# Half of each input load moved from ScalarE's queue to GpSimd's software queue

## The chip, the cores and the metric

The kernel runs on one core of one Trainium2 chip. The metric is the device time of one execution in microseconds (us). A core has a matrix engine (TensorE, in profiles PE, with its weight loads as PEld), three engines for elementwise work (VectorE or DVE, ScalarE or ACT, GpSimd or POOL) and SyncE (SP), which here only issues DMAs. Each engine works through its own instruction stream in order. A DMA is issued by an instruction in the stream of some engine; the transfer itself is done by 16 DMA engines, which all queues share. DMAs issued by SP and ScalarE go through two hardware queues (q1 and q10 in the profile), those issued by GpSimd through a software queue (q0), for which GpSimd writes the descriptors itself.

## The reference, cut to what matters

The input x has 8 batches of 3584 tokens with 192 features. The first step is a causal convolution over 7 tokens, with one set of softmax-normalized weights for each of 8 heads of 24 features. The second step is a mixture of 8 experts: a gate gives each token 8 logits, all 28672 x 8 logits are sorted, and tokens are assigned to experts greedily from the largest logit down, each expert taking at most 3584 tokens. Each token then goes through its expert's two layers with a ReLU between them.

```
w = softmax(weight)                                  # 8 heads x 7 taps
attn[b, s] = sum_k w[h, k] * x_padded[b, s + k]      # per head of 24 features
logits = attn @ w_gate                               # 28672 x 8
for idx in argsort(-logits.flatten()):               # greedy, capacity 3584
    tok, e = idx // 8, idx % 8
    if assigned[tok] < 0 and counts[e] < cap: assigned[tok] = e; counts[e] += 1
out[tok] = relu(attn[tok] @ w1[e]) @ w2[e]
```

## The kernel before, in words

The work falls into two stages that overlap at their border. In the first, some 160 us long, x is read in 16 half batches of 1792 tokens. A half batch lies in SBUF as a tile X of 118 partitions by 16 by 192 floats: 112 partitions hold the tokens of 16 windows, and 6 more hold the tokens ahead of each window. The convolution of a head is one multiplication of TensorE by a Toeplitz matrix TH (function `conv`, tile cv in PSUM, four of them in turn), and ScalarE copies each result from PSUM into a tile a. When all 8 heads are done, ScalarE issues the store of a into a DRAM buffer attn (L214; 1344 KB). VectorE transposes a (tile aT), TensorE computes the gate's logits from it (tile pl), and ScalarE and VectorE bring them into a table LT.

Beside that, from the fourth half batch on, VectorE and TensorE search for a threshold of the logits and build the first lists of tokens (class `Route`: `thresh`, `settle`, `count`, `place`, `sort`). These steps are placed between the convolutions by a planner (`Pace`, `Meter`, `Steps.hook`) that sums costs when the program is built; the order on each engine is then fixed. In the same way the weights of the first expert are loaded into tiles raw by SP (`wload`, L1235 to L1240) and split into a high and a low part by ScalarE and VectorE (`wsplit`).

In the second stage, the rest of the time, tokens are gathered by expert with indirect DMAs of GpSimd (L1308), go through the two layers on TensorE (tiles ph and y), and are scattered to the output, again by GpSimd (L1383).

Inputs are loaded by `load` (L183 to L200). There are four buffers X, so input i takes the buffer of input i - 4. Input 0 is loaded by SP in one piece. For each other input, GpSimd clears the first six rows of an even one (L188), SP loads the six rows ahead of the windows (L189 or L192) and the first 8 of the 16 windows (L194), and the second 8 windows go into a list `later`, from which they are issued a little further on:

```
def part(eng, w, n):
    eng.dma_start(t[6:118, w:w + n], bass.AP(tensor=x.tensor, offset=o + w * W * D, ap=[[D, W], [W * D, n], [1, D]]))
...
    part(nc.sync, 0, 8)
    later.append(partial(part, A, 8, 8))
```

Here A is ScalarE, P is GpSimd, and each half is 112 partitions of 8 rows of 768 bytes, 672 KB. The main loop (L1648) loads input i + 3 ahead of the convolution of half batch i, and issues the second half at once (L1651, L1652); for input 3 it is issued in the middle of half batch 0 (L1663). Since input i + 3 takes the buffer of input i - 1, all its loads wait for the convolution that has just ended. So in ScalarE's stream stand, one after the other: the last evictions of half batch i - 1, its store, the second half of input i + 3, and the first evictions of half batch i.

GpSimd has little to do in the first stage: constants, a part of the Toeplitz matrix, the six rows of each even input, and then, before the first gather, the memset of a weight tile dl (L1192) and of xg (L1306).

Of the kernel before, what the change touches and what calls it, by code (L numbers as in the profile page):

```python
# [114 lines left out]
def build(ctx, tc, nc, x, weight, wg, attn, LT, wk):  # L115
# [4 lines left out]
    V, A, PE, P = nc.vector, nc.scalar, nc.tensor, nc.gpsimd  # L120
# [62 lines left out]
    def load(i, later=None):  # L183
        t = X[i] = k.xp[i % 4].tile([118, 16, D], F32, name="X")
        b, hf = divmod(i, 2)
        o = x.offset + (b * 3584 + hf * 1792) * D
        if hf == 0:
            P.memset(t[0:6, 0], 0.0)  # L188
            nc.sync.dma_start(t[0:6, 1:16], bass.AP(tensor=x.tensor, offset=o + (W - 6) * D,  # L189
                                                    ap=[[D, 6], [W * D, 15], [1, D]]))  # L190
        else:
            nc.sync.dma_start(t[0:6], bass.AP(tensor=x.tensor, offset=o - 6 * D, ap=[[D, 6], [W * D, 16], [1, D]]))  # L192
        def part(eng, w, n):
            eng.dma_start(t[6:118, w:w + n], bass.AP(tensor=x.tensor, offset=o + w * W * D, ap=[[D, W], [W * D, n], [1, D]]))  # L194

        if later is None:
            part(nc.sync, 0, 16)
        else:
            part(nc.sync, 0, 8)
            later.append(partial(part, A, 8, 8))  # L200

    def conv(i, mid, hold=None):
        t = X.pop(i)
# [37 lines left out]
    def logits_t(i):  # L241
# [5 lines left out]
        A.activation(o, v, AF.Copy)  # L247

    k.load, k.conv, k.transp, k.logits, k.logits_t = load, conv, transp, logits, logits_t
    k.toeplitz, k.gate_load, k.gate_ops = toeplitz, gate_load, gate_ops  # L250
    return k
# [1519 lines left out]
```

## Time and profile before

| | |
|---|---|
| median of three runs | 1243.67 us (1243.0 to 1246.95) |
| profiled execution | 1241.13 us, of which the span from the first to the last instruction is 1239.3 us |
| granted TensorE clock, mean | 0.997 |
| busy time of TensorE | 1204.1 us (97% of the span) |
| weight loads / VectorE / ScalarE / GpSimd | 1034.1 / 985.6 / 559.8 / 532.7 us |
| DMA moved | 182.00 MB, mean 147 GB/s |
| loads by L194 on SP / on ScalarE | 15 of 672 KB and one of 1344 KB / 15 of 672 KB |
| issue of a load by L194 on ScalarE | 319 to 1933 ns, median 427 |

A row of a time line reads: start in us, duration in us, engine, line, operation, tile written and tile read, partitions by elements, number of instructions merged into the row, and in brackets the idle time of the engine before it with what ended it. An engine's name with a q (ACTq, SPq) marks its queue of issues. Line 56 is that of a helper through which most instructions pass, so the tiles' names tell the operations apart; the name X is both that of the inputs and, with a number, of work tiles of the lists. The chain of waits is followed back from the last instruction: each row is what the next one waited for.

### The profile page before, as it was taken

To read this page: it belongs to the slowest core of one execution; us is meant where nothing else is said; L and a number is where in the kernel's file an instruction comes from. 1 tells how busy PE (TensorE), PEld (TensorE's weight loads), DVE (VectorE), ACT (ScalarE), POOL (GpSimd) and SP (SyncE) were. 2 spreads that over 40 slices of the span, in tenths; PEclk is the share of its full clock that TensorE was granted. 3 is DMA by queue.
4 is the path that set the end of the run, shared out by engine and by line. 5 is a ranking of instruction groups with operands and counts; after the bars stand their busy time and mean duration, and the time that the engine had idled before them with its cause. 6 is when DMAs were issued, how large, how long until landed. Compare 5 with 4: busy or idle time off the path is not lost.

```text
span 1239.3 us, 21782 instructions
## 1 busy us (share of the span) xinstructions
PE 1204.1 (97%) x7694; PEld 1034.1 (83%) x7694; DVE 985.6 (80%) x2126; ACT 559.8 (45%) x1251; POOL 532.7 (43%) x520
## 2 busy tenths in 40 slices
PE   5999899999999999999999999999999999999997
PEld 2545578889989988889888889999999999999997
DVE  7498679898998999889979866777777777777772
ACT  4544555556445455444554443343333433343332
POOL 2000234435555545555464435434534444543522
PEclk9999999999999999999999999999999999999999
DMA  9999674659426473746343442114223222413100
GB/s 244 372 344 323 193 223 123 141 174 315 146 76 214 135 238 108 238 150 190 100 130 102 129 106 74 42 39 159 93 101 105 100 98 96 154 64 132 48 23 29
DMA packets 128580, 182.00 MB, mean 147 GB/s; under 512 B 20992, under 2 KB 91088, under 8 KB 126800
## 3 DMA queue, kind: packets, MB, share of 16 engines
q1 hardware_dynamic: 85856, 104.13, 27.5%
q0 software_dynamic: 21504, 44.07, 11.9%
q10 hardware_dynamic: 21104, 32.34, 7.7%
q8 instruction: 62, 1.02, 0.3%
q14 instruction: 54, 0.44, 0.1%
HBM read 102.37 MB, written 78.12 MB: 146 GB/s over the span
## 4 chain that ended last, share of the span: by engine, by line
PE 86%; DMA 7%; DVE 4%; issue 1%; ACT 1%; SPq 0%; ACTq 0%; POOL 0%; POOLq 0%; DVEq 0%
PE ph L56 41%; PE y L56 39%; DMA X<-in_x_dram 4%; PE bg L56 3%; PE cv L56 2%; DMA attn<-a 2%; DVE TH L56 1%; PE pl L56 1%; DVE X L56 1%; DMA X<-otab 0%; DVE aT L56 0%; DVE hl L56 0%; DMA raw<-in_moe_w_dram 0%; PE px L56 0%; DMA wb<-in_weight_dram 0%
## 5 line engine op out<-in xcount | busy, mean ns | idle before, releaser
L56 PE MATMUL y<-w,hh 128*128 128x384 f32 x1792 | 535.6, 355 | 0.0
L56 ACT ACTIVATE hh<-ph 128x512 fp32r<-128x512 f32 x448 | 267.6, 597 | 458.1 <-PE ph L56 398.2
L56 PE MATMUL y<-w,hl 128*128 128x192 f32 x1792 | 448.9, 251 | 0.0
L56 DVE SCALAR_TENSOR_TENSOR hl<-ph,hh 128x512 fp32r<-128x512 f32 x448 | 307.9, 687 | 132.0 <-ACT hh L56 110.8
L56 PE MATMUL ph<-xa,w 128*128 128x512 f32 x1344 | 395.2, 402 | 0.4 <-issue 0.4
L56 PEld LDWEIGHTS y<-w,hl 128*128 128x128 f32 x1792 | 340.9, 190 | 16.2
L56 PEld LDWEIGHTS y<-w,hh 128*128 128x128 f32 x1792 | 336.3, 188 | 19.5 <-issue 1.5
L1383 POOL DMA_INDIRECT out_dram<-yo,ia x128 | 145.2, 1134 | 234.2 <-DVE yo L56 197.1
L56 PEld LDWEIGHTS ph<-xa,w 128*128 128x128 f32 x1344 | 218.4, 189 | 21.5 <-issue 2.0
L1383 POOL DMA_INDIRECT out_dram<-yo,ib x96 | 94.9, 988 | 221.0 <-DVE yo L56 213.6
L56 PE MATMUL ph<-xd,w 128*128 128x512 f32 x448 | 177.4, 396 | 0.0
L1308 POOL DMA_INDIRECT xg<-attn,ja x128 | 140.4, 1097 | 79.6 <-issue 38.5
L56 PE MATMUL ph<-xd,dl 128*128 128x512 f32 x448 | 174.2, 389 | 0.2 <-issue 0.2
L56 DVE STREAM_TRANSPOSE xs<-xg 32x128 f32<-32x128 f32 (+2 forms) x408 | 164.8, 404 | 6.6
L56 ACT ACTIVATE yt<-y 128x192 f32<-128x192 f32 x224 | 73.0, 326 | 103.1 <-PE y L56 85.0
L56 PE MATMUL cv<-X,TH 118*128 118x384 f32 x256 | 101.4, 522 | 17.8 <-DVE TH L56 11.9
L1308 POOL DMA_INDIRECT xg<-attn,jb x96 | 103.6, 1079 | 29.3 <-issue 29.3
L56 DVE TENSOR_TENSOR yo<-y,yt 128x192 f32<-128x192 f32 x224 | 79.2, 354 | 42.4 <-ACT yt L56 39.3
L56 PEld LDWEIGHTS ph<-xd,dl 128*128 128x128 f32 x448 | 84.2, 188 | 20.2 <-issue 0.5
L56 PEld LDWEIGHTS ph<-xd,w 128*128 128x128 f32 x448 | 84.0, 187 | 19.6 <-issue 0.6
L56 PEld LDWEIGHTS cv<-X,TH 118*128 118x128 f32 x256 | 45.3, 197 | 48.5 <-POOL TH L152 11.7
L56 ACT ACTIVATE a<-cv 128x384 f32<-128x384 f32 x128 | 58.2, 494 | 47.1 <-PE cv L56 15.7
(237 smaller groups left out, 919.7 us busy)
## 6 DMA issues: line engine op xcount, KB each, us to landing
attn<-a ACTq DMA_DIRECT2D x16, 1344.0 KB
raw<-in_moe_w_dram SPq DMA_DIRECT2D x56, 192.0 KB
X<-in_x_dram SPq DMA_DIRECT2D x15, 672.0 KB
X<-in_x_dram ACTq DMA_DIRECT2D x15, 672.0 KB
kw<-w SPq DMA_DIRECT2D x36, 256.0 KB
kv<-w SPq DMA_DIRECT2D x24, 384.0 KB
scr<-xs SPq DMA_DIRECT2D x96, 96.0 KB
w<-kw SPq DMA_DIRECT2D x6, 1536.0 KB
```

Of the source, the lines that this page charges most:

```text
L56: return f(*a, **k)
L1308: self.nc.gpsimd.indirect_dma_start(out=t[:, b], out_offset=None, in_=self.attn[0:rows], in_offset=bass.IndirectOffsetOnAxis(ap=idx[b], ax ...
L1383: st = self.nc.gpsimd.indirect_dma_start(out=self.out, out_offset=bass.IndirectOffsetOnAxis(ap=idx, axis=0), in_=o, in_offset=None, bounds ...
```

## The change

One line of `load` is changed. The second half of an input is issued by GpSimd on the software queue if the input's number is above 3, and by ScalarE otherwise. That concerns 12 loads, inputs 4 to 15; the halves of inputs 1, 2 and 3 stay on ScalarE. The moment of the call in the program does not change, nor do the bytes and the tiles.

```diff
             part(nc.sync, 0, 8)
-            later.append(partial(part, A, 8, 8))
+            later.append(partial(part, P if i > 3 else A, 8, 8))
```

## The prediction

> **What bounds the kernel now.** I read the busy share by slices first, then the busy time by stages, then the time lines of TensorE, ScalarE and VectorE in the first 160 us, and last the chain of waits there. The slice line and three stages (columns: PE, PEld, DVE, ACT, POOL busy, granted clock, DMA share, GB/s):
>
> ```profile
> DMA  9999674659426473746343442114223222413100
> ...
> 0.00:60.00 60.00, 44.88 (x294) 23.45 (x295) 35.52 (x91) 29.81 (x76) 11.18 (x41) 1.00 1.02 306
> 60.00:94.00 34.00, 31.32 (x266) 16.22 (x265) 31.21 (x85) 16.18 (x45) 0.69 (x2) 1.00 1.05 347
> ...
> 200.00:400.00 200.00, 198.36 (x1255) 177.47 (x1254) 180.53 (x398) 107.09 (x240) 100.07 (x86) 1.00 0.58 173
> ```
>
> From about 160 us on TensorE has hardly a gap (198.36 of 200 us), and the edited line belongs to the loading of the inputs, which is over before that. So the change can only shift the moment at which that dense stage begins; what it is worth is read before 160 us. There, three things are near full at once: TensorE, VectorE (31.21 of 34 us from 60 to 94), and the DMA engines (share 1.02 to 1.05). Next, TensorE's time line: its waits in brackets, with what ended them.
>
> ```profile
> 25.23 4.14 PE L56 MATMUL cv<-X,TH 118*128 118x384 f32 x12 [2.21 <-ACT a L56]
> ...
> 39.93 1.56 PE L56 MATMUL cv<-X,TH 118*128 118x384 f32 x4 [0.34 <-ACT a L56]
> ...
> 48.24 1.56 PE L56 MATMUL cv<-X,TH 118*128 118x384 f32 x4 [0.66 <-ACT a L56]
> ...
> 64.29 0.17 PE L56 MATMUL bg<-m_x,ones 128*128 128x24 bf16 x1 [0.80 <-DVE m_x L56]
> 64.66 1.56 PE L56 MATMUL cv<-X,TH 118*128 118x384 f32 x4 [0.19 <-ACT a L56]
> ...
> 73.44 1.56 PE L56 MATMUL cv<-X,TH 118*128 118x384 f32 x4 [0.86 <-ACT a L56]
> ...
> 81.95 1.56 PE L56 MATMUL cv<-X,TH 118*128 118x384 f32 x4 [0.83 <-ACT a L56]
> ...
> 134.19 0.91 PE L56 MATMUL cv<-X,TH 118*128 118x384 f32 x2 [0.27 <-ACT a L56]
> 135.48 0.91 PE L56 MATMUL cv<-X,TH 118*128 118x384 f32 x2 [0.38 <-ACT a L56]
> ...
> 146.14 0.33 PE L56 MATMUL pt<-ident,L 128*128 128x128 f32 x1 [2.52 <-issue]
> 146.31 3.60 PE L56 MATMUL cv<-X,TH 118*128 118x384 f32 x6
> ```
>
> TensorE has four PSUM tiles for the convolution, and it stops when ScalarE does not evict them. Why ScalarE is late stands in its own time line; L214 is the store of a half batch, L194 the second half of an input:
>
> ```profile
> 21.00 0.32 ACTq L214 DMA_DIRECT2D attn<-a  x1
> 24.32 0.32 ACTq L194 DMA_DIRECT2D X<-in_x_dram  x1
> 24.69 2.63 ACT L56 ACTIVATE a<-cv 128x384 f32<-128x384 f32 x6 [3.72 <-DMA X<-in_x_dram]
> ...
> 38.94 0.32 ACTq L194 DMA_DIRECT2D X<-in_x_dram  x1
> ...
> 44.38 0.32 ACTq L214 DMA_DIRECT2D attn<-a  x1
> ...
> 60.29 1.55 ACTq L214 DMA_DIRECT2D attn<-a  x1
> 62.17 1.84 ACTq L194 DMA_DIRECT2D X<-in_x_dram  x1
> 64.12 2.02 ACT L56 ACTIVATE a<-cv 128x384 f32<-128x384 f32 x5 [3.86 <-DVE X L56]
> ...
> 126.23 0.32 ACTq L214 DMA_DIRECT2D attn<-a  x1
> 126.59 0.60 ACT L56 ACTIVATE X<-bg 128x512 bf16<-128x512 f32 x1 [2.36 <-PE cv L56]
> ...
> 133.13 0.63 ACT L56 ACTIVATE w<-raw 128x512 fp32r<-128x512 f32 x1 [1.41 <-DMA raw<-in_moe_w_dram]
> ```
>
> Input 4's second half stands between the store of half batch 0 and the evictions of half batch 1. The store is out at 21.32, the load only at 24.32, and the evictions behind it start at 24.69. The same happens at 62.17 for input 9. What the load waits for is in the chain of waits:
>
> ```profile
> 46.03 16.06 DMA X<-in_x_dram
> 62.17 17.10 DMA X<-in_x_dram
> 79.37 1.93 ACTq L194
> ...
> 114.37 13.25 DMA attn<-a
> 127.63 5.41 DMA raw<-in_moe_w_dram
> ```
>
> The load issued at 46.03 lands at 62.09, and at 62.17 the next one goes out; that lands at 79.27, and at 79.37 the next goes out. The load does not wait for its buffer (that half batch was convolved by then) but for the landing of the load two half batches earlier. Four issues on SP and ScalarE make up a half batch, so I read this as a ring of eight outstanding hardware issues; it is an inference from the times. So ScalarE is held by the pace of the DMA engines, through an instruction that has nothing to do with its own work.
>
> **What the change takes off ScalarE.** Twelve issues (inputs 4 to 15) leave ScalarE's stream. TensorE's waits for ScalarE just behind them are 2.21 (at 25.23), 0.34, 0.66, 0.19, 0.86 and 0.83: together 5.09 us. Not all of it can be had:
>
> ```profile
> 52.32 0.38 DVE L56 TENSOR_REDUCE M<-LT 128x16 f32<-128x128 f32 x1 [4.38 <-ACT LT L56]
> ...
> 84.24 0.18 DVE L56 TENSOR_REDUCE t_mx<-bg 128x3 f32<-128x24 f32 x1 [0.53 <-PE bg L56]
> ...
> 93.96 0.37 DVE L56 TENSOR_REDUCE M<-LT 128x16 f32<-128x128 f32 x1 [0.91 <-ACT LT L56]
> ```
>
> Before 60 us VectorE idles 4 us in each half batch (4.38 at 52.32), so the first three waits, 2.21 + 0.34 + 0.66 = 3.21 us, reach the end of that stretch in full. From 60 to 94 VectorE runs the threshold search without a gap but the 0.53 at 84.24; the matmuls of that search wait for it (0.80 at 64.29). If TensorE comes earlier there, it waits for VectorE instead: of 0.19 + 0.86 + 0.83 = 1.88 us only the 0.53 is gained. The 0.91 at 93.96 becomes shorter but opens nothing, since TensorE's last count of the search was already paced by VectorE. That makes 3.74 us at 94.
>
> **What it does to the ring.** With three hardware issues a half batch instead of four, the eighth issue back is older by two thirds of a half batch, and it is another one. The last weight load went out at 127.63, when the store issued at 114.37 had landed; it kept ScalarE waiting 1.41 us at 133.13 and TensorE 0.27 + 0.38. After the change it stands eight behind a small row load of input 15, which has long landed. I count 0.65 us gained. In turn the store of half batch 12 (126.23) will stand eight behind the store of 11, which landed at 127.62: a new wait of up to 1.4 us, with evictions queued behind it on ScalarE and TensorE behind those. Below nothing it cannot be. I take 0, since ScalarE was idle 2.36 us right there (126.59) and the store of 11 no longer shares its queue with input 15's half; 1.4 stays in the range.
>
> **What it adds on GpSimd.** The profile has no plain load on the software queue. The nearest rows are its row gathers, of 128 rows of 768 B each; and, behind what is moved, GpSimd's own stream:
>
> ```profile
> L1308 POOL DMA_INDIRECT xg<-attn,ja x128: 994/1012/1995, 140.6 to 726.3; - x128
> ...
> L56 DVE TENSOR_TENSOR oa<-irep,q x64: 648/684/894, 106.6 to 724.3; 128x1024 bf16<-128x1024 bf16 x64
> ...
> 102.98 0.25 POOL L188 MEMSET X<- 6x192 f32 x1 [16.83 <-PE pt L56]
> 103.28 0.95 POOL L1192 MEMSET dl<- 64x1024 f32 x1
> ...
> 140.60 1.25 POOL L1308 DMA_INDIRECT xg<-attn,ja  x1 [35.57 <-DVE ja L56]
> ```
>
> Half an input is 112 partitions of 8 rows, 896 rows of 768 B: seven gathers' worth. The bounds are 0.3 us (an issue that costs what the hardware queue's does, 0.32) and 14 us (seven of the slowest gather, 1.995). I take 7, seven of the undisturbed 0.994, since the gather is the software queue's only row. GpSimd waits for the input buffer as ScalarE did, and it idles 16.83 us between two memsets there. Queued behind each issue are the memset of the next even input, for which SP waits with that input's first rows and first half; the memset of dl (103.28), first read in the dense stage; and the first gather, which waits for VectorE until 140.60. At 7 us an issue fits into a half batch of 8 to 9 us, and all of these keep their time: nothing on the path. Above a half batch it is otherwise; that is the rival that ends slower. VectorE beside the software queue: its oa operations stay at 684 ns in the median and 894 at most, among gathers, so I add nothing for it.
>
> **The sum.** 3.21 + 0.53 + 0.65 = 4.39 us, or 4.4, against the profiled execution: 1241.13 us (span 1239.3), so 1236.7 for a like one. The median of the three runs shown is 1243.67, 2.5 above that execution; taking the same 4.4 from it gives 1239.3. A difference within 0.3% (3.7 us) can hardly be told from none on this kernel, so the forecast lies just beyond that.
>
> **Rivals.** *The DMA engines set the pace.* They are never idle until 125 us, and nothing is taken from them. Input 4's first half was down about when the issue at 38.94 came free, and half batch 4 starts near 44.4 (store at 44.38): 5.5 us of slack. The forecast uses 2.55 of them there. Now three queues share the engines, and the first half has one third of the turns where it had one half against a load. If it slips by more than the remaining 2.9 us, TensorE waits for X itself, and the early gain of 2.21 goes: 4.4 - 2.2 = 2.2 us, 1241.5. Against it: the loads are issued up to 2 us earlier, and the stores no longer stand before them. The Trainium skill, page "DMA: Bandwidth & Descriptors", section "Issuing engines are not separate DMA queues", says that DMAs run on the same 16 engines whoever issues them, so that spreading them saves only issue time. By that rule this rival would hold, with the issue's own wait as the whole gain; the trace agrees so far that the share is above 1 with two queues.
>
> *The wait stays on ScalarE.* The store itself took 1.55 us to issue at 60.29. If it is the fullness of the queue that holds ScalarE, the store takes over the wait: nothing gained, 1243.7. Against it: at 24.32 the load's issue took 0.32 and the time went before it.
>
> *GpSimd falls behind* (slower). Twelve issues of c us from 21 us on end at 21 + 12c; input 15's half lands 17.1 us later, and half batch 15 is convolved from about 147 (in the row of 146.31), 142.6 in the forecast. It turns against the change from c = (142.6 - 21 - 17.1) / 12 = 8.7 us; each us above costs 12. At c = 10, between seven times 0.994 and seven times 1.995, this is 15.6 us: 1254.9. For it: VectorE is full from 60 on, and a gather was once stretched to 1.995. Against: the median is 1.012. The Trainium skill, page "SBUF — State Buffer", section "SBUF: two separate sides", speaks against the change here: an operation of VectorE that takes both ports locks GpSimd out of writing descriptors, and the DMA starves. By that rule c would be stretched wherever VectorE is full; the trace has the stretch, but in few gathers.
>
> **How the numbers follow.** Forecast 0.52, DMA pace 0.20, wait stays 0.13, GpSimd behind 0.15. So faster by over 0.3%: 0.52; within: 0.33; slower: 0.15. The forecast's own range is 1235 to 1240: 1240 is its edge, and 1235 is all 5.09, the 0.65 and the 2.52 us at 146.14 (all engines idle, with no releaser that I can name; I leave it) gone: 8.3 us. The whole range goes from 1235 to 1247: upwards it takes in both cases near no change, the new wait of 1.4 and the highest run of before, 1246.95. It leaves out most of the third rival and little below.
>
> **What would show it.** Right: no L194 on ScalarE after input 3; the evictions of half batch 1 start near 21.5; TensorE's 2.21 at 25.23 is gone and those at 40, 48, 73 and 82 too; VectorE without a gap from 57 to 90; the weight split without a wait for its DMA; GpSimd's issues below 8.5 us; the dense stage 4 us earlier. Wrong: matmuls waiting for a landing of X, stores with issues of 1 us and more, GpSimd busy throughout up to 110 us, or VectorE's operations longer beside GpSimd's issues.

## The result, and the profile after

The changed kernel takes 1258.82 us (median of 4 runs, 1257.29 to 1259.69), the kernel before beside it 1243.96 (1243.0 to 1246.95). The ratio is 1.0111, 95% interval 1.0099 to 1.0123: slower by 14.9 us, outside the predicted range. The profiled execution took 1259.69 us, its span 1257.9. The profiled pair differs by 18.6 us in its spans, 3.7 more than the medians, because the profiled run of before lies 2.8 us under its median and that of after 0.9 above its own.

The waits of TensorE that the change was to remove are gone. In TensorE's time line of the changed kernel (start, duration, instructions, and in brackets the idle time ahead with what ended it) the first three half batches run without the gap of 2.21 us, and the waits for ScalarE at 40, 48, 73 and 82 us have no counterpart:

```profile
19.42 7.98 PE L56 MATMUL cv<-X,TH 118*128 118x384 f32 x24 [0.37 <-DVE TH L56]
...
39.99 1.56 PE L56 MATMUL cv<-X,TH 118*128 118x384 f32 x4
...
47.33 2.90 PE L56 MATMUL cv<-X,TH 118*128 118x384 f32 x4 [5.67 <-DMA X<-in_x_dram]
...
51.17 1.89 PE L56 MATMUL cv<-X,TH 118*128 118x384 f32 x4
...
69.62 0.17 PE L56 MATMUL bg<-m_x,ones 128*128 128x24 bf16 x1 [0.80 <-DVE m_x L56]
...
150.03 0.33 PE L56 MATMUL pt<-ident,L 128*128 128x128 f32 x1 [2.46 <-ACT L L56]
...
161.74 0.97 PE L56 MATMUL ph<-xa,w 128*128 128x512 f32 x3
```

The same matmuls in TensorE's time line of before, the first of half batch 4 and the first of the dense stage:

```profile
43.50 1.45 PE L56 MATMUL cv<-X,TH 118*128 118x384 f32 x4
...
157.43 0.96 PE L56 MATMUL ph<-xa,w 128*128 128x512 f32 x3
```

TensorE arrives 2 us early at half batch 4 and then waits 5.67 us for input 4. It starts it at 47.33 instead of 43.50, and its first four matmuls take 2.90 us instead of 1.45. The stage view has the granted clock (columns as before: busy us of PE, PEld, DVE, ACT, POOL, granted clock, DMA share, GB/s):

```profile
0.00:60.00 60.00, 41.85 (x250) 21.76 (x251) 33.83 (x89) 27.97 (x67) 15.55 (x46) 0.94 0.98 287
60.00:94.00 34.00, 32.23 (x279) 16.72 (x281) 29.21 (x79) 18.03 (x46) 3.94 (x6) 1.00 1.03 341
...
45.00:50.00 5.00, 2.67 (x4) 1.17 (x4) 0.95 (x2) 0.49 (x1) 0.00 (x0) 0.51 0.99 318
```

After the pause TensorE works at about half clock for a few us (0.51 between 45 and 50 us); matched matmul by matmul it is then 6.0 us behind before. By the first matmul of the dense stage 4.3 us are left (161.74 against 157.43).

The dense stage, from there to the last matmul, lasts 1079.1 us against 1074.6. And behind the last matmul (ended at 1240.82 and 1232.02) the span runs on for 17.1 us instead of 7.2. What fills most of that time are two instructions of GpSimd's queue. They raise the software queue's semaphores at the branch that is not taken (L1740), and drain the queue (L1766). The groups of these lines, durations in ns as min/median/max, in before:

```profile
L1740 POOLq INC_SWDGE_SEM  x1: 670/670/670, 1234.1 to 1234.1; - x1
...
L1766 POOLq DRAIN  x3: 40/107/3545, 1234.8 to 1239.0; - x3
```

and in the changed kernel:

```profile
L1740 POOLq INC_SWDGE_SEM  x1: 2201/2201/2201, 1246.6 to 1246.6; - x1
...
L1766 POOLq DRAIN  x3: 46/103/8241, 1248.8 to 1257.6; - x3
```

So the spans' 18.6 us are 4.3 in the first stage, 4.5 in the dense one and 9.8 at the end. The prediction had terms for the first only.

Why was input 4 late? GpSimd's time line shows that its issues are cheap and early, input 5's half at 26.42, input 6's at 33.84:

```profile
21.83 1.10 POOL L194 DMA_DIRECT2D X<-in_x_dram  x1
26.42 0.86 POOL L194 DMA_DIRECT2D X<-in_x_dram  x1 [3.49 <-PE cv L56]
...
33.84 0.83 POOL L194 DMA_DIRECT2D X<-in_x_dram  x1
41.85 0.83 POOL L194 DMA_DIRECT2D X<-in_x_dram  x1 [7.18 <-PE pt L56]
```

SP's time line of the changed kernel, where L189 is the row load of inputs 4 and 6 and L194 their first half:

```profile
24.37 0.27 SPq L189 DMA_DIRECT2D X<-in_x_dram  x1
24.68 0.75 SPq L194 DMA_DIRECT2D X<-in_x_dram  x1
...
37.17 7.44 SPq L189 DMA_DIRECT2D X<-in_x_dram  x1
44.65 3.81 SPq L194 DMA_DIRECT2D X<-in_x_dram  x1
```

and the issues for input 4 in that of before:

```profile
20.51 0.27 SPq L189 DMA_DIRECT2D X<-in_x_dram  x1
20.83 1.22 SPq L194 DMA_DIRECT2D X<-in_x_dram  x1
```

Two things changed. Input 4's loads on SP are issued 3.9 us later. And its first half, issued at 24.68, needs 22.40 us to land by the chain of waits, at 47.08 (before: issued at 20.83, its completions end at 38.92); SP's issues grow to several us behind it. The queues between 25 and 35 us (packets, MB, share of DMA time) in before:

```profile
q10 hardware_dynamic: 1637, 2.61, 72.3%
q1 hardware_dynamic: 1418, 1.06, 34.7%
```

and in the changed kernel:

```profile
q10 hardware_dynamic: 944, 1.98, 54.0%
q0 software_dynamic: 348, 1.37, 36.4%
q1 hardware_dynamic: 576, 0.43, 14.2%
```

SP's queue q1, which carries the first halves, moves 0.43 MB instead of 1.06. Three suspects follow: the late issue, the competition of the software queue, and, at the end, the loads themselves or their number.

### The profile page after: what moved, and what is told of

Read it like the earlier page. It is cut to its first block, busy times and chain, and to the rows that moved or that the text cites. A ratio compares the mean times of both kernels' runs of the same rounds, so it can differ in the third digit from the quotient of the medians.

```text
span 1257.9 us, 21789 instructions
## 1 busy us (share of the span) xinstructions
PE 1208.0 (96%) x7694; PEld 1036.5 (82%) x7694; DVE 983.8 (78%) x2126; ACT 561.5 (45%) x1251; POOL 542.1 (43%) x532
## 4 chain that ended last, share of the span: by engine, by line
PE 84%; DVE 7%; DMA 3%; issue 2%; ACT 1%; another core or an unknown queue 0%; POOL 0%; POOLq 0%; DVEq 0%; SPq 0%
PE ph L56 39%; PE y L56 37%; PE cv L56 4%; PE bg L56 3%; DMA X<-in_x_dram 3%; DVE X L56 2%; DVE aT L56 1%; PE pl L56 1%; DVE hl L56 1%; DMA raw<-in_moe_w_dram 0%; PE px L56 0%; DVE yo L56 0%; POOL TH L152 0%; DMA wb<-in_weight_dram 0%
## 5 line engine op out<-in xcount | busy, mean ns | idle before, releaser
L56 PEld LDWEIGHTS y<-w,hl 128*128 128x128 f32 x1792 | 340.9, 190 | 16.2
L56 ACT ACTIVATE a<-cv 128x384 f32<-128x384 f32 x128 | 61.0, 490 | 46.6 <-PE cv L56 38.7
```

Source lines behind the costliest of these rows:

```text
L56: return f(*a, **k)
```

## The experiments

Each kernel was timed beside runs of before in the same batch. The level of before moved between batches (medians of 1231.7 to 1243.9 us), so times are compared within a batch. `A` is ScalarE, `P` GpSimd; the condition in the line of the change is all that differs where no other diff is shown.

**The end: number of DMAs, or loads?** In the built program the DMAs raise eight completion semaphores in turn, hardware and software DMAs eight each, and a DMA waits for the one eight places back. I shall call them lanes. Twelve more software DMAs shift the lanes by four, and that was the first theory for the longer end. `late8` has `P if i > 7 else A`; `moved_pad4` is the change, `pad4` the kernel before, each with four tiny software loads:

```diff
+            if i == 9:
+                for j in range(4):
+                    nc.gpsimd.dma_start(lst.tile([1, 8], F32, name="pad%d" % j), wg[0:1, :])
```

> Only inputs 8 to 15 move, so 8 more software DMAs than before instead of 12. Theory: the end of the program depends on the number of software DMAs modulo 8 (eight completion lanes in turn), so with 8 more the 17 us behind the last matmul fall back to the 7.3 us of before; and inputs 4 to 7 stay on ScalarE, so the wait of 5.67 us for input 4 at 47 us is gone. 1242 to 1246 us. Rival, the end is prolonged by loads on the software queue as such, whatever their number: 16 to 17 us behind the last matmul, 1252 to 1254 us.

> The change, and four loads of 32 bytes on the software queue ahead of half batch 9, into tiles that nobody reads: 16 more software DMAs than before. Theory: the end falls back to 7.3 us, the first stage stays 4 us behind; 1249 us, and 1244.5 if the 4.5 us lost between 160 and 730 us come from the lanes too. Rival, the loads as such prolong the end: 1258 us.

> The kernel before with the same four loads of 32 bytes on the software queue ahead of half batch 9, no input moved: 4 more software DMAs. Theory: the end takes 17 us instead of 7.3 with nothing else changed; 1253 to 1254 us, up to 1258 if the lanes also cost the 4.5 us between 160 and 730 us. Rival, it is the moved loads: no change, 1244 us.

Measured: `late8` 1.0049 of before (1.0030 to 1.0067), `moved_pad4` 1.0116 (1.0088 to 1.0143), `pad4` 1.0019 (1.0004 to 1.0033). The theory fell in all three. Behind the last matmul stand 10.8 us in `late8` (7.3 expected), 17.05 in `moved_pad4` (7.3 expected) and 7.6 in `pad4` (17 expected). So it is the loads. `late8` loses some 5.3 us in the medians, 3.2 of them at the end (10.8 against the 7.6 of `pad4`); the rest is not assigned. The two lines in `late8`:

```profile
L1740 POOLq INC_SWDGE_SEM  x1: 1677/1677/1677, 1238.1 to 1238.1; - x1
...
L1766 POOLq DRAIN  x3: 46/103/6117, 1239.8 to 1246.5; - x3
```

The profiled execution of `pad4` took 1253.3 us, 7 more than its median, so only its end is read from it; where the 2 us of its median lie is open.

Next came other numbers of loads, `late10` (`i > 5`) and `late11` (`i > 4`); the same loads in smaller pieces, `moved_rows`; and a longer program on GpSimd without a load, `pool_nops`, which is before with 24 memsets of 32 bytes:

```diff
-            later.append(partial(part, P if i > 3 else A, 8, 8))
+            later.append(rows if i > 3 else partial(part, A, 8, 8))
...
+        def rows():
+            for w in (8, 9):
+                P.dma_start(t[6:118, w:16:2], bass.AP(tensor=x.tensor, offset=o + w * W * D, ap=[[D, W], [2 * W * D, 4], [1, D]]))
```

> Inputs 6 to 15 move, 10 loads. The work at the end (raising the software queue's semaphores, and the drain behind it) took 4.2 us before, 7.8 us with 8 loads, 10.4 us with 12: 9.1 us expected with 10. Whether it starts only 3.8 us after the branch, behind the last scatter's landing, as with 12 loads, or at once as with 8: 15.5 or 12.1 us behind the last matmul. Inputs 4 and 5 stay on ScalarE, so no wait for input 4; 5 us slower than before with the early start, 8 with the late one.

> Inputs 5 to 15, 11 loads. The raising of the semaphores takes 2.07 us and the drain 7.7. If the late start comes with a number of rows in the software queue, it sets in here or at 12: 13 or 16.5 us behind the last matmul.

> The change, but each software load as two, of the even and of the odd windows, so that two rows of 768 bytes never lie side by side in SBUF: 24 software loads, the same bytes and the same number of rows. Theory: a packet of the software queue holds six rows because they lie side by side; now it holds one, the software queue gets no more turns' worth of bytes than SP's queue, the first half of input 4 lands earlier and TensorE's wait for it falls from 5.67 to 2 or 3 us. If the work at the end goes by rows, the 17 us behind the last matmul stay, 1255 to 1256 us in all; if it goes by software loads, they grow to 24 us, 1262 us. Rival, the packet's size has no part in it: the wait stays at 5 to 6 us.

> The kernel before, with 24 memsets of 32 bytes more on GpSimd at half batch 9, no DMA more. If the late start at the end comes from the length of GpSimd's program (the changed kernel fetched one block of instructions more), the raising of the semaphores starts 3.8 us late here too and the span's end moves 1.5 to 2 us away from the last matmul; if it comes from what lies in the software queue, it starts at once and the end takes 7.3 to 7.6 us.

`late10` measured 1.0061 (1.0043 to 1.0079; 8.4 us in the medians where 5 were expected, since a wait for an input comes on top, told below), `moved_rows` 1.0099 (1.0080 to 1.0117), and one execution each of `late11` 1240.3 us (before: 1232.57) and of `pool_nops` 1240.6 (before: 1241.85). Their ends, with those of kernels told of further below:

| kernel | software loads of an input's half | raising us | longest drain us | raising starts after the last matmul us | end us |
|---|---|---|---|---|---|
| before | 0 | 0.67 | 3.55 | 2.1 | 7.2 |
| pool_nops | 0 | 0.67 | 3.53 | 2.1 | 7.7 |
| four_pool | 1 | 0.81 | 3.40 | 2.1 | 7.5 |
| both45 | 4 | 1.18 | 4.07 | 2.1 | 8.2 |
| late8 | 8 | 1.68 | 6.12 | 2.1 | 10.8 |
| late10 | 10 | 1.94 | 7.18 | 2.1 | 12.1 |
| late11 | 11 | 2.06 | 7.67 | 2.1 | 12.7 |
| the change | 12 | 2.20 | 8.24 | 5.8 | 17.1 |
| moved_turn | 12 | 2.20 | 8.24 | 4.9 | 16.2 |
| moved_pad4 | 12, and 4 tiny ones | 2.22 | 8.32 | 5.6 | 17.1 |
| moved_rows | 24 of half the size | 2.21 | 8.32 | 5.5 | 16.9 |
| moved_and_two | 13 | 2.33 | 8.73 | 5.6 | 17.5 |
| both_pool | 24 | 2.42 | 9.22 | 5.4 | 17.9 |

Each load adds 0.13 us to the raising, (2.20 - 0.67) / 12, and from 8 to 12 loads 0.53 us to the drain, (8.24 - 6.12) / 4. Twice the loads of half the size cost the same, and four tiny loads add 0.03 us to the raising (0.70 in `pad4`), so the number of issues does not set it. The bytes alone do not either: `rows_pool`, told of below, moves only 0.15 MB more on the software queue than before and raises for 0.79 us, about as long as `four_pool` with one load of 672 KB. What it goes by is open. From 13 to 24 loads raising and drain hardly grow. With one or two loads the drain ends no later than SP's own last steps (both at 1238.4 in before) and costs nothing.

In the kernels with 12 loads and more the raising also starts 2.8 to 3.7 us late. The 9.8 us are thus about 1.5 + 4.7 + 3.7. In the changed kernel the late start is 0.2 us behind the landing of the last scatter (1246.60 and 1246.43), but in `moved_turn` the raising starts at 1233.11, ahead of that landing at 1233.66, so it does not wait for it. The cause is not settled, and it need not be the loads. TensorE's sequencer, VectorE and SP stand still at this branch in every kernel, SP for 3.5 us in before; in the six kernels with the late start GpSimd does so too. These six, the changed kernel and the last five rows of the table, are also the only ones of all the runs whose pages count 55 packets on q14, a queue that the profile calls one of instructions. In before, and in the changed kernel:

```profile
q14 instruction: 54, 0.44, 0.1%
```

```profile
q14 instruction: 55, 0.45, 0.1%
```

`pool_nops` starts at once with as many rows of GpSimd in its trace as the changed kernel, but it has 54 such packets too. So a pause for the loading of GpSimd's program is a rival that no run tested; if it holds, the 3.7 us come from where the program happens to be cut and not from the loads.

**The first stage: off ScalarE, but not on the software queue.** `on_sp` has `nc.sync if i > 3 else A`.

> The second half of inputs 4 to 15 issued by SP, behind the first half, instead of by ScalarE or GpSimd: it leaves ScalarE but stays on a hardware queue, and the count of software DMAs is that of before. Theory (the prediction's reading of the waits was right, and the software queue is what hurts): TensorE's waits for ScalarE ahead of 60 us, 3.2 us, go, no wait for input 4 takes their place, the end takes 7.3 us; 1239.5 to 1241. Rival, a load that leaves ScalarE for any other place is held up in a way that costs the same: 1243 to 1248.

Measured 1.0088 (1.0060 to 1.0115): the theory fell, the rival held, and it cost more than that said. Input 4's first half lands in time, at 39.03, but the second half, now behind it on the same queue, only at 44.34. TensorE's time line in `on_sp`:

```profile
44.59 2.77 PE L56 MATMUL cv<-X,TH 118*128 118x384 f32 x4 [3.37 <-DMA X<-in_x_dram]
...
97.08 1.53 PE L56 MATMUL cv<-X,TH 118*128 118x384 f32 x4 [2.09 <-DMA X<-in_x_dram]
...
140.26 1.65 PE L56 MATMUL cv<-X,TH 118*128 118x384 f32 x2 [6.32 <-ACT a L56]
```

The end is 7.6 us there, but SP, which now issues both halves, falls behind: two loads take it 2.8 to 6.4 us to issue, the first weight load goes out at 125.50 instead of 113.46, and ScalarE's time line shows the bill:

```profile
138.71 0.63 ACT L56 ACTIVATE w<-raw 128x512 fp32r<-128x512 f32 x1 [8.69 <-DMA raw<-in_moe_w_dram]
```

**Late issue, or competition?** SP's row load of input 4 is late in the changed kernel because it now stands eight places behind the second half of input 2, which lands at 24.3; before, ScalarE's load for input 4 stood there. `moved_turn` adds one tiny hardware load, which moves the lanes on by one. `moved_and_two` puts the second half of input 2 on the software queue as well (`P if i == 2 or i > 3 else A`).

```diff
         k.gate_load()
+        nc.sync.dma_start(lst.tile([1, 8], F32, name="turn"), wg[0:1, :])
```

> The change, and one load of 32 bytes on SP's queue just behind the gate's weights, which moves every later hardware DMA on by one completion lane. Theory: the row load of input 4 waited for the second half of an earlier input only because the two share a lane when ScalarE's issue is left out; with the lanes moved on it is issued at 20.5 to 21 us instead of 24.4, its first half lands some 3.5 us earlier, and TensorE waits about 2 us for it instead of 5.67: 1255 us. Rival, the packets of the software queue alone hold the first half up: TensorE waits as long as in the changed kernel, 1258 to 1259 us.

> The change, and the second half of input 2 on the software queue too, so that SP's loads of inputs 3 and 4 inherit no late lane and are issued at 17 to 18 and 20.5 to 21 us. If the late issue made TensorE's wait for input 4, it falls from 5.7 us to under 2, and the kernel is 3 to 4 us faster than the changed one on the same chip (ratio to before 1.008 to 1.009 instead of 1.0115). If the packets of the software queue starve the first half whenever it is issued, the wait stays at 4 us or more and the ratio at 1.011 to 1.012. The end takes 17 to 18 us in both.

`moved_turn` (1.0115, 1.0094 to 1.0137) missed its aim: the lane passed to SP's first half of input 3, issued at 24.50 instead of 18.33, and TensorE waited 9.33 us for input 3. `moved_and_two` did what it was to do. Its SP issues input 4 on time, yet the first half lands at 47.56, and TensorE waits no less:

```profile
21.27 0.27 SPq L189 DMA_DIRECT2D X<-in_x_dram  x1
21.58 0.31 SPq L194 DMA_DIRECT2D X<-in_x_dram  x1
```

```profile
47.69 2.90 PE L56 MATMUL cv<-X,TH 118*128 118x384 f32 x4 [5.87 <-DMA X<-in_x_dram]
```

The ratio is 1.0101 (1.0085 to 1.0116). So the late issue is not what makes the 5.67 us; the competition is. ScalarE's stores, which now go out earlier, are not enough for it: they go out as early in `on_sp`, where the first half, issued at 25.28 with no software load beside it, lands at 39.03. `moved_rows` was also to test the packets' size, but the edit did not change it (382 packets for 1.37 MB between 25 and 35 us, 3.6 KB each), so it says nothing on that; its waits are 1.79 us for input 3 and 4.18 for input 4. In `late10` and `late11` TensorE waits too, for the second input that moves (4.28 us for input 7, 3.93 for input 6), and in `late8` for none.

If the half on SP's queue is starved beside software loads, the wait goes when that half joins them (`both_pool`). `four_pool` has `P if i == 4 else A`.

```diff
-            part(nc.sync, 0, 8)
+            part(P if i > 3 else nc.sync, 0, 8)
```

> Both halves of inputs 4 to 15 on the software queue, only the six rows stay on SP: 24 software loads. Theory (beside software loads the hardware queue gets too small a share, so the half left on SP lands late): no half is left behind, TensorE's wait for input 4 falls from 5.7 us to under 2; the work at the end doubles, 18 us instead of 10.4, behind the late start: 24 to 26 us behind the last matmul; 1.014 to 1.016 of the time before. Rival, the loads are late because the DMA engines are full, whatever the queue: the wait stays at 4 us or more, 1.018 and up.

> Only the second half of input 4 on the software queue. Theory: one load of 672 KB outruns the first half of input 4 once, TensorE waits 2 to 5 us for it; the end takes 7.6 us; 1.002 to 1.004 of the time before. Rival, it takes the stream of software loads, with that of input 5 ahead of input 4's first half: no wait for input 4, the 2.2 us gained behind half batch 0 stay, 0.998.

`both_pool` takes 1.0064 (1.0041 to 1.0086). TensorE's waits up to 160 us there (us in all, times, longest):

```profile
PE cv L56 <- DVE TH L56: 13.2, 2, 12.2
PE cv L56 <- ACT a L56: 1.9, 1, 1.9
PE bg L56 <- DVE m_x L56: 1.4, 3, 0.8
```

No wait for an input is left, though both halves of 12 inputs ride on the software queue. It loses 7.6 us against before, but its end alone is 10.4 us longer (17.9 against 7.5 in `four_pool`, of the same batch), so the rest of it gains about 2.8. My 24 to 26 us for its end were wrong, as the work there stops growing. In `four_pool` the rival held: with one software load there is no wait for input 4, and it is the one version whose interval lies below 1, if only just: 0.9986 (0.9973 to 0.9999), 1.3 us in the medians. It takes the stream: issued at nearly the same moment (25.27 and 24.68), the first half lands at 42.04 here and at 47.08 in the changed kernel. There the software halves of inputs 5 and 6, needed some 8 and 16 us after input 4, had landed by 36.2 and 42.7 us, ahead of input 4's first half. That no wait is seen in `four_pool` is in part luck: TensorE is held for 4.03 us by ScalarE just before and would else have come to input 4 shortly before it landed. That wait is what `four_pool` loses again, and it is in ScalarE's time line, at its load of input 6, which inherits the lane of a store:

```profile
40.63 0.33 ACTq L194 DMA_DIRECT2D X<-in_x_dram  x1
41.08 1.64 ACT L56 ACTIVATE a<-cv 128x384 f32<-128x384 f32 x4 [6.72 <-DMA attn<-a]
```

**Is there a version that keeps the gain?** `four_sp`: only input 4 on SP (`nc.sync if i == 4 else A`), with the tiny load of `moved_turn`. `two_pool`: `P if i == 2 else A`. `rows_pool`: the gate's weights and the six rows of inputs 2 and 3 by GpSimd, no half moved (`P if i in (2, 3) else nc.sync` in L189 and L192, `P` in L168). `both45`: both halves of inputs 4 and 5 by GpSimd. `four_six`: `P if i in (4, 6) else A`.

> The kernel before with the small load that moves the lanes on, and only the second half of input 4 issued by SP; all else stays on ScalarE, nothing more on the software queue. Theory: the wait of TensorE for ScalarE behind half batch 0, 2.2 us, goes, row and first half of input 4 are issued as early as before, no wait for input 4 appears: 2 us faster than before, 1241.5 to 1242. Rival, SP's queue is held back by ScalarE's larger packets whatever the moment of issue: a wait for input 4 of 2 us or more takes the gain, 1243 to 1245.

> The kernel before, with only the second half of input 2 issued by GpSimd; inputs 4 to 15 stay on ScalarE. Theory: what held a load until 24.5 us was the completion lane of that half of input 2, which the eighth hardware DMA after it inherits (ScalarE's load for input 4 before, SP's row load of input 4 in the changed kernel, SP's first half of input 3 where the lanes were moved on by one). On the software queue that half holds no such lane: TensorE's wait of 2 us for ScalarE behind half batch 0 goes, no wait for an input takes its place, one software load is too few to prolong the end (7.3 us): 2 us faster than before. Rival, the wait was for the bytes and not for the lane, or the software queue's packets hold up the first half of input 2 or 3: no faster, or slower by a wait for input 2 or 3.

> The kernel before, with three small loads on the software queue instead of SP's: the gate's weights (6 KB) and the six rows of inputs 2 and 3 (72 KB each at most). No half of an input moves. The completion lane of the second half of input 2 then passes to the row load of input 5, issued at 28 us, instead of to ScalarE's load for input 4. Theory: TensorE's wait of 2 us for ScalarE behind half batch 0 goes, nothing is starved, the end takes 7.5 us: 0.998 of the time before. Rival, the next lanes hand the wait on, to ScalarE's load of input 5 or to a first half: 1.000 or above.

> Both halves of inputs 4 and 5 on the software queue, all else as before: 4 software loads. Theory: TensorE's wait of 2 us for ScalarE behind half batch 0 goes, no half is left behind a stream, so no wait for an input; ScalarE's load of input 6 inherits the lane of store 0, landed by then. The work at the end takes 5.2 us (2.55 and 4 times 0.66), about 1 us past the landing that covered it: 0.999 of the time before, between 0.998 and 1.000. Rival, the ScalarE wait comes back at a later lane, as in the kernel with only input 4 moved: 1.000 to 1.003.

> The second halves of inputs 4 and 6 on the software queue, all else on ScalarE. Theory: with only input 4 moved, ScalarE's load of input 6 inherited the lane of store 1 and TensorE waited 4 us for ScalarE at 41 us; with that load moved too nothing of ScalarE waits there, two software loads with 15 us between them do not outrun SP's queue, and the work at the end, 3.9 us, stays behind the last landing (7.5 us in all): 0.997 of the time before, faster than with input 4 alone (0.9986). Rival, input 6's software half outruns its first half or SP's row load of input 7, which now inherits store 1's lane, comes late: a wait for input 6 or 7 of 2 us or more, 0.999 to 1.002.

All five are slower: `four_sp` 1.0044 (1.0027 to 1.0060), `two_pool` 1.0022 (1.0012 to 1.0031), `rows_pool` 1.0024 (1.0006 to 1.0043), `both45` 1.0016 (1.0007 to 1.0025), `four_six` 1.0048 (1.0034 to 1.0062). The 2 us at 25 us are gained in each (also in `two_pool` and `rows_pool`, where the load for input 4 stays on ScalarE and only the place eight issues back has another owner), and a later load inherits the wait: input 3's first half in `four_sp` (TensorE waits 3.36 us), ScalarE's load of input 5 in `two_pool` and `rows_pool` (TensorE waits 4.65 and 4.72 us for the evictions behind it), input 3 and ScalarE's load of input 6 in `both45` (1.61 and 2.86). In `four_six` a second software load, issued at 33.8 us, is enough to bring back the wait for input 4 that `four_pool` does not have: the first half lands at 44.93 instead of 42.04, and TensorE, not held by ScalarE before it, is there at 41.2:

```profile
45.18 2.04 PE L56 MATMUL cv<-X,TH 118*128 118x384 f32 x4 [3.98 <-DMA X<-in_x_dram]
```

**The dense stage.** `before_again` is before, unchanged, for a second profile.

> The kernel before, unchanged, for a second profile: the first one, at 1241.1 us, lies under the median of its runs. The end takes 7.3 us again; where the dense stage is about 3 us slower than in the first profile, those 3 us are no part of the change's cost.

It took 1230.16 us, where the median of its batch was 1231.68. Its dense stage, from first ph to last matmul, lasts 1068.3 us; in the same batch it lasts 1068.2 in `moved_turn` and 1068.4 in `moved_rows`, both with all 12 halves on the software queue. So in that batch the change costs the dense stage nothing. In the batch of `pad4` and `on_sp` it lasts 1077.6 us in `on_sp` and 1079.4 in `moved_pad4`. The 4.5 us of the first pair may be scatter in the main, since its profiled runs lie 3.7 us further apart than the medians; that the scatter falls into this stage is inferred, and 0.8 us are not assigned.

## Why the prediction was wrong, point by point

Two steps failed. The forecast took it that the first half of an input would land within its slack beside the software loads, and its sum had no term for what runs behind the last matmul.

**What the change takes off ScalarE: the waits went, the gain was not kept.** The reading that TensorE waits for ScalarE, and ScalarE for a landing eight issues back, stands: every kernel whose load for input 4 left ScalarE has no gap at 25 us. In `both_pool`, where no wait for an input is left, about 2.8 us show of the 3.74 (to 94 us) that were forecast.

**"What it does to the ring" stopped half way.** It asked which wait goes when the eighth issue back changes, for two places late in the stage, and not who stands at the eighth place behind the slow load at the beginning. That was SP's row load of input 4, held till 24.37. In the changed kernel this is not what costs the time (`moved_and_two`), but such a place handed on is what undid most of the versions that were to keep the gain. The 0.65 us at the weight split came, the two waits of TensorE are gone, but not for the reason given. The last weight load did not go out early. It waited longer, for a store, as the row of SP and the line of SP's waits from 110 to 140 us in the changed kernel show:

```profile
132.43 0.47 SPq L1238 DMA_DIRECT2D raw<-in_moe_w_dram  x1
```

```profile
SPq L1238 <- DMA attn<-a: 11.4, 1, 11.4
```

That load lands 3.1 us later than before (136.13 against 133.05), in a stage that runs 4.4 us later, and ScalarE comes to it at 136.21. So that these waits are gone is owed to the delay, which is luck.

The 0 taken for the new wait of store 12 held: TensorE has no wait there.

**"What it adds on GpSimd": 7 us an issue was eight times too much.** The group of L194 in the changed kernel:

```profile
L194 POOL DMA_DIRECT2D X<-in_x_dram x12: 826/826/1098, 21.8 to 117.4; - x12
```

A plain load of 896 rows takes 0.83 us, less than the gather of 128 rows that I measured it by. So GpSimd never falls behind, and the rival that ended slower, at 1254.9 us, had the right sign with the wrong mechanism; that its time is near the measured one is luck. No issue took longer than 1.10 us, and from 60 to 94 us, where VectorE is busy 29.21 of 34 us, none took longer than 0.96. The lock that the Trainium skill describes for operations of VectorE that take both ports (page "SBUF — State Buffer", section "SBUF: two separate sides") is not seen in these issues. The cheap issue may be part of the harm, since with it GpSimd is ahead of SP; no run tried a dearer one.

**"The DMA engines set the pace" was the right rival for the first stage, at too low a chance and too low a price.** It allowed 2.9 us of slack and, beyond that, the loss of the early gain of 2.21. The first half landed at 47.08, 8 us later than before, and TensorE paid 5.67 us and 2.2 of half clock (3.8 us behind before at the first matmul of half batch 4, 6.0 some 5 us on): 4.3 us lost at the dense stage instead of 2.2 gained. The failing step is the sentence that gave the first half "one third of the turns" and did not ask how much a turn carries. Counted in packets, q1 got 576 of 1868 between 25 and 35 us, 31%, near that third. In bytes it got 0.43 of 3.78 MB, 11%; before it had 1.06 of 3.67, 29%. A packet of q0 carries 3.9 KB there (1.37 MB by 348), one of q1 0.75 (0.43 MB by 576). The Trainium skill, page "DMA: Bandwidth & Descriptors", section "Queues, rings and completion order", says that an engine goes round its queues packet by packet and drains a whole packet, of several descriptors, before it switches. The shares of bytes go that way, but q0 and q1 did not get equally many packets, and no run here changed the packet's size, so how the engines choose is not shown.

**"The sum" left out the end of the program.** About two thirds of the loss, 9.8 of 14.9 us, lie behind the last matmul: 6.2 in the raising and the drain, rows that stood in the trace of before with 0.67 and 3.55 us, and 3.7 in the late start, whose cause is open. The prediction took it that behind the dense stage nothing can depend on the loads. It costed the issue, the transfer and the waits of a software DMA, not the closing of its queue.

**The range** could not hold the result, since its upper end came from cases near no change, and the only slow case had the wrong cause.

## What to carry to other kernels

A transfer moved to another queue can take bandwidth from the queue that carries its partner: where the DMA engines are full, ask which of the transfers that are needed together lands last, and move both or neither. A wait for a completion eight issues back does not vanish with its instruction; list who stands at that place afterwards. And add the closing of a queue to its price: look at what runs behind the last useful instruction, and whether it grows with the use of the queue.

## What the runs showed of the hardware

The raising and the drain together, which close the software queue, grow by 0.66 us for each load of 672 KB from 8 to 12 of them, and are 11.6 us (2.42 + 9.22) with 24. A plain software load of 896 rows is issued in 0.83 us, an indirect one of 128 rows in 1.01. After a pause of 5.67 us TensorE's granted clock was 0.51 between 45 and 50 us and 0.81 between 50 and 55; after the 2.21 us of before it stayed at 1.00, but `before_again` was at 0.66 between 25 and 30 us after a pause of 2.0, so a pause of that length costs clock in one run and not in another.
